# Permuting the closing factors inside SBUF, and two sums made by accumulating transfers, in a fused convolution and FFN kernel

## The chip, the cores and the metric

One Trainium2 chip, one of its cores. The metric is device time in microseconds: 2329.91 us is the median of three runs of the kernel before (2326.67 to 2331.57). The profiled execution, from which all rows below come, took 2344.11 us, of which 2342.3 us lie between its first and last instruction. About 0.2% is what a measurement of this kernel can tell from no change.

## The reference

Two stages run one after the other on 8 x 4096 = 32768 rows of 192 features.

```python
w = exp(weight_gen - max over K);  w = w / (sum over K + 1e-9)       # 8 heads, K = 7 taps
out[b, s, h, :] = sum over k of w[b, s, h, k] * x_pad[b, s + k, h, :] # 24 features a head, causal
h = out.reshape(32768, 192) @ w_in                                    # 192 -> 2048
g = max(h, 0) ** 2
y = g @ w_out                                                         # 2048 -> 192
```

## The kernel before, in words

The rows are cut into 64 chunks (`c`), each of 4 rows in each of 128 partitions. For a chunk the kernel makes the weighted sum over seven taps (the convolution), turns the result so that features lie in the partitions, splits it into a high and a low part, and runs the two matrix products with both parts, so that the result is close to float32.

**The convolution of a chunk** is VectorE work on tiles `pr` of 128x768: seven products (`mul`, L387) and six sums (`add`, L400). It is spread over the steps of the two chunks ahead of the one that uses it. `turn` (L488) transposes the sum in blocks of 32 into `xr`; four transfers on SyncE's queue write it to DRAM as `xd` (L494), two more read it back as `xT` in the layout wanted (L499). ScalarE then makes the high part `xh` (L428) and VectorE the low part `xl` (L431), three pieces each.

**A chunk's main loop** has eight steps `j`. In each step TensorE makes two blocks of the first product (`mm1`, L523) and two of the second (`mm2_scaled`, L604 to L614) for work that is two steps older. ScalarE does relu, square and the high part of the result, VectorE the low part (L560). At step 1 the second product of the chunk before ends. `sum_turned` then frees its four PSUM banks: ScalarE copies two of them, VectorE adds the other two (L651), part 0 first and part 1 later in the step. The second product of the next chunk cannot begin until these adds are done.

**Part 1** holds the last 64 features as two half sums, in partitions 0 to 63 and 64 to 127. L653 moves the upper half down by a transfer on SyncE's queue; at step 4 VectorE adds it (L667) and transposes the result (L668).

**The closing factor.** Chunks 6 to 62 are called scaled: their rows are scaled by powers of two, and at the end each output row is multiplied by a factor twice (`close_scaled`, L687). The factor is one number for each partition, made once for two chunks at step 2 of the even chunks (`factor`). As the output has its partitions permuted, so must the factor be: GpSimd's queue writes 128 numbers to a DRAM tile `fd` (L284), and when this has landed reads them back by four transfers in the other order (L288). The table `SCALED_SLOTS` says how many entries of the convolution's list each step takes, and `N_AHEAD` how many of them stand ahead of `sum_turned` at step 1.

**What sets the order.** Each engine and each queue runs its instructions in the order in which the program issues them. An instruction that waits holds all that is behind it on its engine or queue. Chunks 1 to 3 already let transfers accumulate (`moved`, L405).

Of the kernel before, what the change touches and what calls it, by code (L numbers as in the profile page):

```python
# [8 lines left out]
F32 = mybir.dt.float32  # L9
# [5 lines left out]
ALU = mybir.AluOpType  # L15
# [15 lines left out]
def kernel(  # L31
# [9 lines left out]
    nc = tc.nc  # L41
# [4 lines left out]
    P = 128  # L46
    Q = 32
# [8 lines left out]
    D1 = 64  # L56
# [6 lines left out]
    LAG = 2  # L63
    CONV_BEG = 1
    CONV_SLOTS = (2, 1, 4, 1, 3, 0, 3, 3, 0, 3)
    SCALED_SLOTS = (2, 1, 4, 1, 2, 1, 3, 2, 3, 1)
    OUT_STEP = 3
    LOAD_STEP = 5
    NBUF = NF // 2
    FIRST = 6  # L70
    GL_POOL = 5
    SCALE_STEP = NJ
    N_AHEAD = 3

    const = ctx.enter_context(tc.tile_pool(name="const", bufs=1))
    stage = ctx.enter_context(tc.tile_pool(name="stage", bufs=3))
# [4 lines left out]
    op = ctx.enter_context(tc.tile_pool(name="op", bufs=1))  # L81
    dram = ctx.enter_context(tc.tile_pool(name="dram", bufs=2, space=bass.MemoryType.DRAM))
# [6 lines left out]
    def put_out(c, t0, t1, o_sb, reads):  # L89
        rows = slice(rows_of(c) + t0, rows_of(c) + t1)  # L90
        if reads == 0:
            nc.sync.dma_start(out=out.rearrange("(p r) d -> p r d", r=R)[:, rows, :], in_=o_sb[:, t0:t1])
            return
        if reads == 3:
            v = out.rearrange("(q a b r) d -> b q a r d", q=P // Q, a=P // Q, r=R)
            n = v.shape[0] // 4
            for k in range(4):
                nc.sync.dma_start(out=v[k * n:(k + 1) * n, :, :, rows, :], in_=o_sb[k * Q:(k + 1) * Q, t0:t1])
            return
        v = out.rearrange("(q a b r) d -> q b a r d", q=P // Q, a=2 ** reads, r=R)  # L100
        for q in range(P // Q):
            nc.sync.dma_start(out=v[q, :, :, rows, :], in_=o_sb[q * Q:(q + 1) * Q, t0:t1])
# [7 lines left out]
    def is_scaled(c):  # L110
        return FIRST <= c < NCH - 1
# [167 lines left out]
    def factor(gi):  # L279
        f = att.tile([P, 1], F32, name="x_fac", bufs=2)  # L280
        x_out[gi] = fo = att.tile([P, 1], F32, name="x_out", bufs=3)
        nc.vector.tensor_tensor(out=f, in0=x_pow[gi], in1=v_unroot, op=ALU.mult)  # L282
        fd = dram.tile([P, 1], F32, name="fd")
        nc.gpsimd.dma_start(out=fd, in_=f)  # L284
        v = fd.rearrange("(q a b) e -> b q a e", q=P // Q, a=P // Q)
        n = v.shape[0] // 4
        for k in range(4):
            nc.gpsimd.dma_start(out=fo[k * Q:(k + 1) * Q], in_=v[k * n:(k + 1) * n])  # L288

    def peak_w(k):  # L290
        nc.vector.tensor_reduce(
# [37 lines left out]
    def conv_steps(c, on_pe, moving=False):  # L329
# [3 lines left out]
        n = TC * H  # L333
        wf = wt[:, lo:lo + TC].rearrange("p t h k -> p (t h) k")
        if c < N_PE:
            e = eps[c]
# [5 lines left out]
        parts = xts[c] = {}  # L342
# [28 lines left out]
        def product(k):  # L371
            if on_pe and k < 3:
                if "spare" not in parts:
                    parts["spare"] = att.tile([P, 2, TC, D], F32, name="spare", tag="xT")
                return att.tile([P, TC, D], F32, name="prx", tag="xr") if k == 2 else parts["spare"][:, k]
            if moving and k == 4:
                return att.tile([P, TC, D], F32, name="prw", tag="wide")
            return att.tile([P, TC, D], F32, name="pr", bufs=4)

        def mul(k, t0=0, t1=TC):  # L380
            def f():
                if k not in prs:
                    prs[k] = product(k)
                m = (t1 - t0) * H
                src = xt[:, lo + k + t0:lo + k + t1, :].rearrange("p t (h g) -> p (t h) g", h=H)
                dst = prs[k][:, t0:t1, :].rearrange("p t (h g) -> p (t h) g", h=H)
                tt(out=dst, in0=src, in1=wf[:, t0 * H:t1 * H, k:k + 1].broadcast_to([P, m, G]), op=ALU.mult)  # L387
            return f
# [9 lines left out]
        def add(k, k0=0):  # L398
            def f():
                tt(out=prs[k0], in0=prs[k0], in1=prs.pop(k), op=ALU.add)  # L400
            return f

        def moved(k, k0):
            def f():
                nc.gpsimd.dma_start(out=prs[k0], in_=prs.pop(k), accum_op=ALU.add)  # L405
            return f

        def both(*fs):
            return lambda: [f() for f in fs]

        def taps():
            if moving:
                return [mul(0), both(mul(1), moved(1, 0)), mul(2), both(mul(3), moved(3, 2)),
                        both(mul(4), moved(4, 0)), mul(5), mul(6), add(5, 6), add(2, 6), add(6)]
            fs = [mul(0), mul(1)]
            for k in range(1, K):
                if k + 1 < K:
                    fs.append(mul(k + 1))
                fs.append(add(k))
            return fs  # L420
# [60 lines left out]
        def turn():  # L481
# [16 lines left out]
            for h in range(2):  # L498
                nc.sync.dma_start(out=xT[h * D1:(h + 1) * D1], in_=xd.rearrange("(k p) n -> p k n", p=D1))  # L499

        return steps + taps() + [turn], splits


# [139 lines left out]
    def sum_turned(c, parts=(1, 0)):  # L643
        acc = accs[c]
        if c not in works:
            works[c] = stage.tile([P, 3, N], F32, name="raw")
        X = works[c]
        for k in parts:
            nc.scalar.copy(X[:, k], acc[2 * k])  # L649
        for k in parts:  # L650
            nc.vector.tensor_tensor(out=X[:, k], in0=acc[2 * k + 1], in1=X[:, k], op=ALU.add)  # L651
        if 1 in parts:
            nc.sync.dma_start(out=X[0:D1, 2], in_=X[D1:P, 1])  # L653

    def store_turned(c, part):
        X = works[c]

        def blocks(v):
            return v.rearrange("p (a t i) -> p t a i", a=P // Q, t=TC) if is_scaled(c) else v

        if part == 0:
            o_sb = op.tile([P, TC, D], F32, name="o_sb", bufs=2)
            Y = stage.tile([P, 2, N], F32, name="raw")
            outs[c] = o_sb, Y
            nc.vector.transpose(blocks(Y[:, 0]), X[:, 0])
        else:
            nc.vector.tensor_tensor(out=X[0:D1, 1], in0=X[0:D1, 1], in1=X[0:D1, 2], op=ALU.add)  # L667
            nc.vector.transpose(blocks(outs[c][1][0:D1, 1]), X[0:D1, 1])  # L668
        o_sb, Y = outs[c]
        y = Y[:, part].rearrange("p (t q i) -> p q t i" if c < N_PE or is_scaled(c) else "p (q t i) -> p q t i", t=TC, i=Q)  # L670
        for e in range(P // Q if part == 0 else D1 // Q):
            d0 = part * P + e * Q
            if is_scaled(c):
                nc.sync.dma_start(out=o_sb[:, :, d0:d0 + Q], in_=outs[c][1][e * Q:(e + 1) * Q, part])
                continue
            for q in range(P // Q):
                queue = nc.gpsimd if part and c == NCH - 2 else nc.sync
                queue.dma_start(
                    out=o_sb[q * Q:(q + 1) * Q, :, d0:d0 + Q],
                    in_=y[e * Q:(e + 1) * Q, q],  # L680
                )
        if part and not is_scaled(c):
            put_out(c, 0, TC, o_sb, 2)
# [150 lines left out]
    def plan_conv(m, a, b):  # L834
# [5 lines left out]
        elif m > 3:  # L840
            fs = iter(a)
            for j, n in enumerate(SCALED_SLOTS if is_scaled(m) else CONV_SLOTS):
                for _ in range(n):
# [20 lines left out]
    for gi in range(FIRST // CPG, NCH // CPG):  # L864
        at(CPG * gi - 2, 2, lambda gi=gi: measure(gi))
        at(CPG * gi - 2, 3, lambda gi=gi: power(gi))
        at(CPG * gi, 2, lambda gi=gi: factor(gi))
# [8 lines left out]
    for c in range(1, NCH):  # L876
        tail = c == NCH - 1
        for j in range(NJ):
# [28 lines left out]
            if split_sum:  # L907
                for f in fs[:N_AHEAD]:
                    f()
                del fs[:N_AHEAD]  # L910
                sum_turned(done, (0,))
            elif done is not None:
                sum_turned(done)
            for f in fs:
                f()
            if c > 1:
                for part in range(2):
                    if j == (LOAD_STEP if tail else 2 * part + 2 if is_scaled(c - 1) else OUT_STEP + part):
                        store_turned(c - 1, part)
# [4 lines left out]
            if split_sum:  # L924
                sum_turned(done, (1,))
# [5 lines left out]
    c = NCH - 1  # L931
# [56 lines left out]
```

## Time and profile before

| what | value |
|---|---|
| median of 3 runs | 2329.91 us |
| profiled execution | 2344.11 us |
| its span, first to last instruction | 2342.3 us |
| TensorE busy | 2151.8 us (92%) |
| VectorE busy | 1949.2 us (83%) |
| ScalarE busy | 1842.7 us (79%) |
| GpSimd busy | 95.6 us (4%) |
| mean granted TensorE clock | 0.973 |

A busy share is an average over stretches with different limits. A chunk's cycle is best cut at the start of its transpose `xr` (L488), which occurs once in each chunk. A row of a table of stretches has the stretch, its length, the busy time of each engine in it, the granted clock and the share of the DMA engines that was in use. SPq is SyncE's queue of transfers; a transfer's row has the time it was issued, not that it landed.

### The profile page before, as it was taken

To read this page: it belongs to the slowest core of one execution; us is meant where nothing else is said; L and a number is where in the kernel's file an instruction comes from. 1 tells how busy PE (TensorE), PEld (TensorE's weight loads), DVE (VectorE), ACT (ScalarE), POOL (GpSimd) and SP (SyncE) were. 2 spreads that over 40 slices of the span, in tenths; PEclk is the share of its full clock that TensorE was granted. 3 is DMA by queue.
4 is the path that set the end of the run, shared out by engine and by line. 5 is a ranking of instruction groups with operands and counts; after the bars stand their busy time and mean duration, and the time that the engine had idled before them with its cause. 6 is when DMAs were issued, how large, how long until landed. Compare 5 with 4: busy or idle time off the path is not lost.

```text
span 2342.3 us, 49184 instructions
## 1 busy us (share of the span) xinstructions
PE 2151.8 (92%) x19484; PEld 1735.2 (74%) x19484; DVE 1949.2 (83%) x3067; ACT 1842.7 (79%) x3551; POOL 95.6 (4%) x163
## 2 busy tenths in 40 slices
PE   9989899998999999998889988999898999989989
PEld 8878677777777777776767767677676777767778
DVE  9989887977879888788787887888878788888885
ACT  8878777877878777888777787787877878778786
POOL 1000000000000000000000000000000000000000
PEclk9999999999999999999999999999999999999999
DMA  8433334333243342433424334233342433423422
GB/s 214 93 84 65 91 71 97 80 86 72 70 95 80 87 91 56 88 86 89 92 53 85 87 87 92 53 84 89 84 92 53 85 91 85 89 60 78 95 52 57
DMA packets 311296, 195.47 MB, mean 83 GB/s; under 512 B 212000, under 2 KB 269472, under 8 KB 307224
## 3 DMA queue, kind: packets, MB, share of 16 engines
q1 hardware_dynamic: 305128, 188.64, 36.2%
q0 software_dynamic: 5936, 3.68, 1.1%
q8 instruction: 152, 2.49, 0.5%
q14 instruction: 80, 0.66, 0.1%
HBM read 106.54 MB, written 49.56 MB: 67 GB/s over the span
## 4 chain that ended last, share of the span: by engine, by line
DVE 43%; PE 26%; DMA 17%; ACT 5%; issue 5%; SPq 2%; DVEq 0%; another core or an unknown queue 0%; ACTq 0%
PE ph L523 14%; DVE pr L400 10%; DMA xT<-xd 9%; DVE pr L387 9%; DVE du L560 9%; DMA xd<-xr 7%; PE acc L604 6%; DVE xl L431 4%; DVE gl L560 4%; DVE raw L651 3%; PE acc L639 2%; ACT rg L540 2%; PE acc L608 1%; ACT xh L428 1%; ACT rg L547 1%
## 5 line engine op out<-in xcount | busy, mean ns | idle before, releaser
L523 PE MATMUL ph<-xh,W 64*128 64x512 f32 x6096 | 1066.0, 409 | 0.0
L604 PE MATMUL acc<-gh,V 64*128 64x512 f32 x5472 | 796.2, 393 | 160.2 <-DVE raw L651 83.2
L604 PEld LDWEIGHTS acc<-gh,V 64*128 64x128 f32 x5472 | 593.1, 191 | 276.6 <-DVE raw L651 120.6
L523 PEld LDWEIGHTS ph<-xh,W 64*128 64x128 f32 x6096 | 715.8, 190 | 100.2 <-ACT gh L551 13.2
L540 ACT ACTIVATE rg<-ph 128x512 f32<-128x512 f32 x992 | 538.6, 596 | 240.8 <-PE ph L523 234.2
L547 ACT ACTIVATE rg<-rg 128x512 f32<-128x512 f32 x1007 | 580.7, 634 | 0.2
L551 ACT CAST gh<-rg 128x512 fp32r<-128x512 f32 x1008 | 575.6, 625 | 3.0 <-PE acc L581 3.0
L523 PE MATMUL ph<-xl,W 64*128 64x512 f32 x3048 | 491.0, 380 | 0.1
L387 DVE TENSOR_TENSOR pr<-xt,wt 128x768 f32<-128x768 f32 x440 | 418.1, 952 | 2.3
L560 DVE TENSOR_TENSOR gl<-rg,gh 128x512 f16<-128x512 f32 x570 | 390.2, 741 | 25.9 <-ACT gh L551 24.4
L523 PEld LDWEIGHTS ph<-xl,W 64*128 64x128 f32 x3048 | 360.0, 189 | 40.9 <-ACT xl L442 0.5
L431 DVE TENSOR_TENSOR xl<-xT,xh 128x512 fp32r<-128x512 f32 x186 | 122.1, 686 | 305.6 <-ACT xh L428 300.9
L400 DVE TENSOR_TENSOR pr<-pr 128x768 f32<-128x768 f32 x366 | 348.9, 953 | 2.2
L428 ACT CAST xh<-xT 128x512 fp32r<-128x512 f32 x186 | 108.0, 618 | 195.1 <-DMA xT<-xd 195.1
L608 PE MATMUL acc<-gl,du 64*128 64x512 f16 x1140 | 237.3, 390 | 1.0 <-DVE gl L560 1.0
L560 DVE TENSOR_TENSOR du<-rg,gh 128x512 f16<-128x512 f32 x342 | 232.1, 733 | 2.4 <-ACT gh L551 2.4
L608 PEld LDWEIGHTS <-du 64*128 64x128 f16 x1824 | 100.1, 98 | 104.2 <-issue 57.7
L608 PE MATMUL acc<-du 64*128 64x512 f16 x684 | 132.9, 400 | 15.1 <-DVE du L560 14.4
L284 POOL DMA_DIRECT2D fd<-x_fac x29 | 17.1, 589 | 1874.9 <-DVE x_fac L282 1752.4
L614 PEld LDWEIGHTS <-du 64*64 64x64 f16 x1824 | 48.3, 106 | 57.8 <-issue 24.1
L651 DVE TENSOR_TENSOR raw<-acc,raw 128x512 f32<-128x512 f32 x124 | 84.4, 684 | 6.6 <-ACT raw L649 6.6
L649 ACT COPY raw<-acc 128x512 f32<-128x512 f32 x124 | 74.1, 601 | 14.0 <-PE acc L639 9.8
(127 smaller groups left out, 1230.1 us busy)
## 6 DMA issues: line engine op xcount, KB each, us to landing
xT<-xd SPq DMA_DIRECT2D x124, 384.0 KB
xt<-in_x_dram SPq DMA_DIRECT2D x30, 1344.0 KB
out_dram<-o_sb SPq DMA_DIRECT2D x254, 96.0 KB
xd<-xr SPq DMA_DIRECT2D x248, 96.0 KB
o_sb<-raw SPq DMA_DIRECT2D x342, 64.0 KB
raw<-raw SPq DMA_DIRECT2D x62, 128.0 KB
wt<-in_weight_gen_dram SPq DMA_DIRECT2D x31, 224.0 KB
raw<-in_moe_w_in_dram SPq DMA_DIRECT2D x16, 192.0 KB
```

The lines of the kernel that those rows point to most:

```text
L387: tt(out=dst, in0=src, in1=wf[:, t0 * H:t1 * H, k:k + 1].broadcast_to([P, m, G]), op=ALU.mult)
L400: tt(out=prs[k0], in0=prs[k0], in1=prs.pop(k), op=ALU.add)
L428: nc.scalar.copy(parts["h"][:, k, n], src[k][:, n])
L431: tt(out=parts["l"][:, k, n], in0=src[k][:, n], in1=parts["h"][:, k, n].bitcast(F32), op=ALU.subtract)
L523: nc.tensor.matmul(two[i], w, order(xx[rows, k]), start=(n == 0), stop=(n == last))
L540: nc.scalar.activation(r, ph, AF.Relu)
L547: nc.scalar.activation(r, r, AF.Square)
L551: nc.scalar.copy(gh, rgs[c, fb])
L560: nc.vector.tensor_tensor(out=gl, in0=g, in1=h, op=ALU.subtract)
L604: nc.tensor.matmul(acc[b + h], V[rows, fb, e:e + P], two_halves(g[rows]), start=fb == 0 and e < 2 * P, stop=False)
L608: nc.tensor.matmul(acc[h], V16[rows, 2 * j + i, 0:P], gls[c, j][rows, i], start=False, stop=last and i == 1)
L651: nc.vector.tensor_tensor(out=X[:, k], in0=acc[2 * k + 1], in1=X[:, k], op=ALU.add)
```

## The change

Three parts, all in the scaled chunks. The factor no longer goes through DRAM: eight transfers of 16 numbers each, on GpSimd's queue, read every eighth partition of `x_fac` and write 16 partitions of `x_out`. One of the six sums of the convolution (product 3 onto product 2) is made by an accumulating transfer on GpSimd's queue; the products 2 and 3 come first for that, and the list has 19 entries in place of 20. The upper half sum of part 1 is added to the lower by an accumulating transfer on GpSimd's queue; the transfer on SyncE's queue and VectorE's add go.

```diff
-    SCALED_SLOTS = (2, 1, 4, 1, 2, 1, 3, 2, 3, 1)
+    SCALED_SLOTS = (2, 1, 4, 1, 2, 1, 3, 2, 2, 1)
-    N_AHEAD = 3
+    N_AHEAD = 2
@@ factor
-        fd = dram.tile([P, 1], F32, name="fd")
-        nc.gpsimd.dma_start(out=fd, in_=f)
-        v = fd.rearrange("(q a b) e -> b q a e", q=P // Q, a=P // Q)
-        n = v.shape[0] // 4
-        for k in range(4):
-            nc.gpsimd.dma_start(out=fo[k * Q:(k + 1) * Q], in_=v[k * n:(k + 1) * n])
+        n = P // (P // Q) ** 2
+        for b in range(n):
+            nc.gpsimd.dma_start(out=fo[b * P // n:(b + 1) * P // n], in_=f[b::n])
@@ taps
+            if is_scaled(c):
+                return [mul(2), both(mul(3), moved(3, 2)), mul(0), mul(1), add(1), mul(4), add(4), mul(5), add(5), add(2), mul(6), add(6)]
@@ sum_turned
-        if 1 in parts:
+        if 1 in parts and is_scaled(c):
+            nc.gpsimd.dma_start(out=X[0:D1, 1], in_=X[D1:P, 1], accum_op=ALU.add)
+        elif 1 in parts:
             nc.sync.dma_start(out=X[0:D1, 2], in_=X[D1:P, 1])
@@ store_turned
-            nc.vector.tensor_tensor(out=X[0:D1, 1], in0=X[0:D1, 1], in1=X[0:D1, 2], op=ALU.add)
+            if not is_scaled(c):
+                nc.vector.tensor_tensor(out=X[0:D1, 1], in0=X[0:D1, 1], in1=X[0:D1, 2], op=ALU.add)
```

The line numbers in the changed kernel differ by a few: L387 is now L384, L400 is L397, L405 is L402, L431 is L430, L488 is L487, L494 is L493, L499 is L498, L560 is L559, L651 is L650, L653 is L652 (on GpSimd's queue in the scaled chunks), L668 is L670, L674 is L676, L687 is L689, L288 is L285.

VectorE between a transpose `xr` and the first low part `xl`, from the first product of the next convolution on (`gl` is the low part of the result, `raw` holds the output sums). Before:

```order
L387 TENSOR_TENSOR pr<-xt,wt 128x768
L560 TENSOR_TENSOR gl<-rg,gh 128x2x256 x2
L387 TENSOR_TENSOR pr<-xt,wt 128x768
L667 TENSOR_TENSOR raw<-raw 64x512
L668 STREAM_TRANSPOSE raw<-raw 64x4x4x32
L560 TENSOR_TENSOR gl<-rg,gh 128x2x256 x2
L431 TENSOR_TENSOR xl<-xT,xh 128x512
```

After:

```order
L384 TENSOR_TENSOR pr<-xt,wt 128x768
L559 TENSOR_TENSOR gl<-rg,gh 128x2x256 x2
L384 TENSOR_TENSOR pr<-xt,wt 128x768
L670 STREAM_TRANSPOSE raw<-raw 64x4x4x32
L559 TENSOR_TENSOR gl<-rg,gh 128x2x256 x2
L430 TENSOR_TENSOR xl<-xT,xh 128x512
```

The add of the half sums is gone; the two products are now 2 and 3 in place of 0 and 1, and the second is followed by the accumulating transfer on GpSimd's queue.

VectorE from the closing multiplication at step 0 to the two adds that free the PSUM banks. Before:

```order
L687 TENSOR_SCALAR o_sb<-o_sb,x_out 128x768
L387 TENSOR_TENSOR pr<-xt,wt 128x768
L400 TENSOR_TENSOR pr<-pr 128x768
L560 TENSOR_TENSOR gl<-rg,gh 128x2x256 x2
L387 TENSOR_TENSOR pr<-xt,wt 128x768
L400 TENSOR_TENSOR pr<-pr 128x768 x2
L651 TENSOR_TENSOR raw<-acc_16560,raw 128x512
L356 TENSOR_REDUCE mx<-wt 128x32
L357 TENSOR_TENSOR wt<-wt,mx 128x224
L651 TENSOR_TENSOR raw<-acc_16562,raw 128x512
```

After:

```order
L689 TENSOR_SCALAR o_sb<-o_sb,x_out 128x768
L397 TENSOR_TENSOR pr<-pr 128x768 x2
L559 TENSOR_TENSOR gl<-rg,gh 128x2x256 x2
L384 TENSOR_TENSOR pr<-xt,wt 128x768
L397 TENSOR_TENSOR pr<-pr 128x768
L650 TENSOR_TENSOR raw<-acc_16561,raw 128x512
L353 TENSOR_REDUCE mx<-wt 128x32
L354 TENSOR_TENSOR wt<-wt,mx 128x224
L650 TENSOR_TENSOR raw<-acc_16563,raw 128x512
```

One sum less stands ahead of the adds that free the banks; in step 0 a product and a sum have become two sums.

GpSimd's queue where the first scaled chunks begin (the rows on `pr`, `prw` are those of chunks 1 to 3). Before:

```order
L405 DMA pr<-prw 128x768
L405 DMA pr<-pr 128x768 x2
L405 DMA pr<-prw 128x768
L284 DMA fd<-x_fac 128x1
L288 DMA x_out<-fd 32x1x1 x4
```

After:

```order
L402 DMA pr<-prw 128x768
L402 DMA pr<-pr 128x768 x2
L285 DMA x_out<-x_fac 16x1 x8
L402 DMA pr<-pr 128x768
L652 DMA raw<-raw 64x512
L402 DMA pr<-pr 128x768
```

The queue that held five small transfers for two chunks now holds eight small ones, and an accumulating transfer of 128x768 and one of 64x512 for each chunk. From SyncE's queue only L653 is gone, in each scaled chunk; what follows it there, `xd` and `xT`, is in the same order.

## Rows read from the trace of the kernel before

**Rows 1.** The page: the chain that ended last, share of the span.
```profile
DVE 43%; PE 26%; DMA 17%; ACT 5%; issue 5%; SPq 2%; DVEq 0%; another core or an unknown queue 0%; ACTq 0%
```
**Rows 2.** Busy time by stretch: length, engines, granted clock, DMA share, GB/s.
```profile
1006.45:1039.65 33.20, 32.33 (x309) 26.07 (x305) 30.02 (x47) 27.38 (x52) 0.00 (x0) 1.00 0.46 113
1039.65:1078.71 39.06, 32.81 (x307) 25.85 (x305) 30.35 (x50) 29.79 (x59) 2.95 (x5) 1.00 0.29 55
1078.71:1111.38 32.67, 32.07 (x309) 26.11 (x305) 30.14 (x47) 26.94 (x52) 0.00 (x0) 1.00 0.47 115
243.00:2247.11 2004.11, 1829.68 (x16683) 1452.97 (x16680) 1666.78 (x2588) 1574.02 (x3031) 82.76 (x140) 0.97 0.37 81
```
**Rows 3.** SyncE's queue in order of time: start, time to issue, transfer.
```profile
131.94 1.79 SPq L494 DMA_DIRECT2D xd<-xr  x4
136.74 1.33 SPq L499 DMA_DIRECT2D xT<-xd  x2
...
244.06 2.42 SPq L494 DMA_DIRECT2D xd<-xr  x4
254.63 1.31 SPq L499 DMA_DIRECT2D xT<-xd  x2
...
1040.67 2.69 SPq L494 DMA_DIRECT2D xd<-xr  x4
1051.32 1.28 SPq L499 DMA_DIRECT2D xT<-xd  x2
...
1079.71 1.80 SPq L494 DMA_DIRECT2D xd<-xr  x4
1083.25 1.29 SPq L499 DMA_DIRECT2D xT<-xd  x2
...
2208.97 2.11 SPq L494 DMA_DIRECT2D xd<-xr  x4
2219.92 1.28 SPq L499 DMA_DIRECT2D xT<-xd  x2
```
**Rows 4.** GpSimd in order of time, the even chunk's stretch; in brackets the wait before.
```profile
1040.05 0.59 POOL L284 DMA_DIRECT2D fd<-x_fac  x1 [61.25 <-DVE x_fac L282]
1049.40 2.36 POOL L288 DMA_DIRECT2D x_out<-fd  x4 [8.76 <-issue]
```
**Rows 5.** Busy time by stretch, inside the even chunk's stretch.
```profile
1045.00:1050.50 5.50, 5.50 (x54) 4.67 (x51) 5.07 (x8) 4.45 (x9) 1.10 (x2) 1.00 0.00 0
```
**Rows 6.** VectorE in order of time; in brackets the wait before an instruction.
```profile
1058.50 0.69 DVE L431 TENSOR_TENSOR xl<-xT,xh 128x512 fp32r<-128x512 f32 x1 [8.40 <-ACT xh L428]
...
1085.05 0.97 DVE L387 TENSOR_TENSOR pr<-xt,wt 128x768 f32<-128x768 f32 x1
...
1090.98 0.69 DVE L431 TENSOR_TENSOR xl<-xT,xh 128x512 fp32r<-128x512 f32 x1 [2.29 <-ACT xh L428]
...
1092.46 0.95 DVE L400 TENSOR_TENSOR pr<-pr 128x768 f32<-128x768 f32 x1
1093.33 1.35 DVE L560 TENSOR_TENSOR du<-rg,gh 128x512 f16<-128x512 f32 x2
```
**Rows 7.** The chain that ended last, in order of time: start, length, what.
```profile
1011.65 6.98 DMA xT<-xd
...
1051.99 5.78 DMA xT<-xd
```
**Rows 8.** Groups by line: count, busy us, mean ns, idle before.
```profile
L667 DVE TENSOR_TENSOR raw<-raw 64x512 f32<-64x512 f32 x62 | 42.2, 681 | 5.0 <-DMA raw<-raw 5.0
```
**Rows 9.** GpSimd in order of time: the last accumulating transfer of the early chunks.
```profile
84.85 0.86 POOL L405 DMA_DIRECT2D pr<-prw  x1 [3.95 <-DVE prw L387]
```
**Rows 10.** Busy time by stretch, around that transfer.
```profile
86.00:88.50 2.50, 2.50 (x28) 2.19 (x26) 2.47 (x5) 1.97 (x5) 0.00 (x0) 1.00 0.87 157
88.50:89.00 0.50, 0.50 (x8) 0.45 (x6) 0.50 (x1) 0.50 (x2) 0.00 (x0) 1.00 0.00 0
```
**Rows 11.** Who waited for whom, stretch 1078.7 to 1111.4.
```profile
PE acc L604 <- DVE raw L651: 0.6, 1, 0.6
```

## The prediction

> **What bounds the kernel now.** The page's chain comes first: it changes between VectorE (43%), TensorE (26%) and transfers (17%), so no engine bounds alone [rows 1]. I therefore cut the span into the stretches between two transposes `xr`, and the table of stretches shows two kinds in turn. The one that starts in an even chunk takes 39.06 us, its neighbours 33.20 and 32.67 us, though the engines do nearly the same work in each: TensorE 32.81, 32.33 and 32.07 us, VectorE 30.35, 30.02 and 30.14 us [rows 2]. In the short kind TensorE stands still for 32.67 - 32.07 = 0.6 us, and that is its wait for the adds that free the PSUM banks [rows 2, 11]. The short stretch is bound by TensorE; the long one has some 6 us in which nobody is the bound.
>
> Where these 6 us go is read in the queues. In the short stretch the reading of `xT` is issued 3.54 us after the first writing of `xd` (1079.71 to 1083.25), in the long one 10.65 us after it (1040.67 to 1051.32). The first and the last of the 28 long stretches have 10.57 and 10.95 us [rows 3]. SyncE waits there for `xd` to be reported as landed. But the DMA engines move nothing from 1045.0 to 1050.5 [rows 5]: the bytes are through, the report is late. What lies beside it in the even chunks alone is the factor's way through DRAM: `fd` is issued at 1040.05, just ahead of `xd`, and GpSimd sees it landed only at 1049.40, 9.35 us later, for 512 bytes [rows 4]. Chunk 4 is even and has no factor yet: 4.80 us from `xd` to `xT` (131.94 to 136.74) [rows 3]. So I take the write of 128 numbers of 4 bytes to DRAM to be what holds back the reports of `xd`. VectorE pays: it waits 8.40 us for `xl` in the long stretch and 2.29 us in the short one [rows 6].
>
> **The change part by part.**
>
> *Factor.* `fd` goes, in 29 chunks (6, 8, ... 62). If it is the cause, all 28 long stretches become like the short ones. In its place stand eight issues. Four of the old ones took 2.36 us [rows 4], so eight take some 4.7 us of an engine that is 4% busy, from about 1040 to 1045; the next work on that queue is the accumulating transfer after the second product, some 7 us after the transpose. The factor is used first a chunk later. Cost on the path: nothing, if these transfers don't hold up `xd` as `fd` does. They write 4 bytes at a time too, but to SBUF. The nearest row is the four `x_out` transfers, which also write 4 bytes to SBUF: they were issued from 1049.40 to 1051.76, `xT` at 1051.32, and `xT` then took 5.78 us in the chain against 6.98 us where no such transfer was near [rows 3, 4, 7]. So between 0 (by this) and 7 us a long stretch (as `fd`); I take 0.
>
> The Trainium skill, DMA: Bandwidth & Descriptors, section Specifications, gives 512 bytes as the least transfer for full rate and says that anything smaller is done by read-modify-write. By that rule the eight new transfers would be in the same class as `fd`; the two `xT` times above speak against it for SBUF, and the first rival below has its result.
>
> *The convolution's sum.* One add less for VectorE, 0.87 us from start to start in a row of such instructions (1092.46 to 1093.33) [rows 6], and it is one of those between `xl` and the adds that free the banks, so it is on the path from `xl` to the next transpose. Added is a transfer of 384 KB that reads, adds and writes. Its own cost is seen in an early chunk: issued at 84.85, it moved from about 86.0 to before 88.5 [rows 9, 10], so some 3.7 us with 2.2 us of all DMA engines at the 0.87 share. Issued at 1086.02, where the second product ends [rows 6], it is done by about 1090. Its sum is needed only at step 0 of the next chunk, and the tile that it reads is written again by a product of step 7, which comes after the rows shown to 1093.33 + 1.35 = 1094.68 [rows 6]. That cover is over 4 us; without it VectorE would wait for what is over. What it can hit is `xT`: issued at 1083.25, landing some 7 us later [rows 3, 7], so its last 3 us lie beside the accumulation's 2.2 us from about 1087.2. Bounds: 0 and 2.2 us later for `xT`. The bytes of `xT` are the earlier of the two, so I take 0.7 us, of which VectorE's and TensorE's slack (below) leaves little.
>
> *The half sum.* L667 goes, 0.68 us for each chunk [rows 8], but it stands before the wait for `xl` [rows 6]: it turns into waiting, gain 0. The transfer changes to GpSimd's queue and accumulates 128 KB, a third of the one above. It is issued right after the second add that frees the banks, two instructions ahead of the transpose, and the transpose of part 1 that waits for it comes after the product that ends at 1086.02, over 7 us after `xr`. At 3.7 us it is hidden twice over. If it came later than that, VectorE's idle 2.29 us would take the first of it. On SyncE's queue one wait goes ahead of `xd`; `xd` waits for a later VectorE instruction, so nothing is gained.
>
> *The sum.* From the first `xr` in chunk 6 (243.0) to that in chunk 61 (2247.1) lie 55 stretches in 2004.1 us, 36.4 us each, 28 long and 27 short [rows 2]. The new stretch P has two floors. TensorE: 32.07 us. VectorE and the transfers: 12.27 us from `xr` to `xl` (1078.71 to 1090.98) and 20.40 from there to the next `xr` (1111.38) [rows 2, 6], less 0.87: 31.8 us, or 32.5 with the 0.7 us. The wait for the banks, 0.6 us, shrinks with the add that stood ahead of it. I take P = 32.5 us. 55 x 32.5 = 1787.5, which is 216.6 us less. The profiled execution would be 2344.1 - 216.6 = 2127.5 us; it stands 0.6% above the median of the runs (2329.9 / 2344.1 = 0.9939), so the forecast is 2115 us. In the 55 stretches the mean granted clock is 0.97, in the short ones shown 1.00, which is 2.4 GHz throughout [rows 2]; that part of the gain is in P already.
>
> The likeliest case alone: P from 32.07 (TensorE without any wait: 1763.9, so 2103.9, at the median 2091 us) to 33.4 us (1837, so 2177, at the median 2164 us), the short stretch of today with some collision and no gain by the add.
>
> **The rivals.**
>
> *The eight small transfers hold `xd` as `fd` did.* For it: 4 bytes each, the same queue, issued at the same moment as `xd`. Against it: `xT` beside `x_out`, and the target is not DRAM. Then only the add is gained: 0.87 us in 28 long stretches and some 0.5 us in 27 short ones, 38 us: 2306, at the median 2292 us.
>
> *The accumulation takes its full 2.2 us from `xT`.* For it: both run over the same DMA engines and the times touch. Against it: most of `xT` is through by then. P = 31.8 + 2.2 = 34.0 us, 55 x 34.0 = 1870, 134 us less: 2210, at the median 2197 us.
>
> *Slower: the accumulation of the half sum, in flight just ahead of `xd` in every chunk, holds back its report.* Price: the 7.1 us of the long stretch, now in all 55. P = 31.8 + 7.1 = 38.9 us, 2140 us, 135 us more: 2480, at the median 2465 us. It is slower than before from P = 36.4 us on, a delay of 4.6 us a chunk. Against it: in the early chunk the DMA engines are idle 3.7 us after the issue [rows 9, 10], and it writes to SBUF in pieces of 2 KB. The Trainium skill, same page, section Queues, rings and completion order, says that a report is a write that lands only after every earlier write of that DMA engine, across its queues. By that rule the report of `xd` waits for whatever GpSimd's queue has in flight: it is what `fd` shows, and the way by which this rival would come.
>
> **How the numbers follow.** Forecast 0.77, the full collision 0.11, the small transfers 0.07, slower 0.04, and 0.01 that all cancels. The forecast's own range is 2091 to 2164 us. With the collision (2197) it holds 88%, of which some part lies outside: 2085 to 2197 us as the range. Faster by over 0.2%, which is about what a measurement of this kernel can tell from no change: 0.95 (the first three cases); within 0.2%: 0.01; slower: 0.04.
>
> **What would show it.** Right: no more alternation, all stretches near 32.5 us, `xT` issued 3.5 to 5 us after `xd` in even chunks too, no 8 us wait of VectorE for `xl`, TensorE busy about 98% in the stretches. VectorE's adds (now L397) 57 fewer. The step on the factor is wrong if even chunks keep 10 us between `xd` and `xT`; the step on the accumulation is wrong if VectorE's wait for `xl` is above 4 us in all chunks; the step on the half sum is wrong if VectorE waits ahead of the transpose L670. The forecast fails if TensorE, without its long pause, is not fed at the rate of the short stretches.

## The result, and the profile after

The changed kernel takes 2101.8 us (median of four runs, 2101.0 to 2104.7), the kernel before 2328.3 us (median of four): a ratio of the means of 0.9035, with a 95% interval of 0.9007 to 0.9063. The forecast was 2115 us, with 2091 to 2164 us for the likeliest case. The profiled execution has a span of 2100.0 us, 242.3 us less than before.

The page of the changed kernel, its busy times and its chain that ended last:

```profile
PE 2074.4 (99%) x19484; PEld 1707.0 (81%) x19484; DVE 1870.8 (89%) x2953; ACT 1845.2 (88%) x3551; POOL 221.2 (11%) x364
...
PE 71%; DVE 15%; DMA 6%; ACT 4%; issue 2%; SPq 1%; DVEq 0%; ACTq 0%
```

The chain that alternated between VectorE, TensorE and transfers [rows 1] is now for 71% TensorE's own work. The table of stretches of the changed kernel, from one `xr` to the next (L487), has first all 55, then an even chunk, an odd one and an even one; the columns are those of [rows 2], the busy times in the order TensorE, its weight loads, VectorE, ScalarE, GpSimd:

```profile
239.90:2007.30 1767.40, 1757.42 (x16693) 1429.36 (x16692) 1591.98 (x2479) 1574.68 (x3028) 204.04 (x334) 1.00 0.48 103
1075.01:1106.93 31.92, 31.92 (x307) 25.98 (x304) 29.17 (x49) 29.23 (x57) 5.64 (x10) 1.00 0.41 79
1106.93:1139.48 32.55, 32.09 (x310) 26.16 (x306) 28.73 (x45) 28.47 (x56) 1.72 (x2) 1.00 0.53 128
1139.48:1171.43 31.95, 31.92 (x307) 25.99 (x304) 29.06 (x48) 28.87 (x56) 5.63 (x10) 1.00 0.43 80
```

The 39 us of the even chunk are gone: it is now even a little shorter than its neighbour. The 55 stretches take 1767.4 us in place of 2004.1 [rows 2], 32.13 us each; these 236.7 us are nearly all of the 242.3. In them TensorE is busy for 1757.4 us, 99.4%, at a granted clock of 1.00 (2.4 GHz), where the mean was 0.97 before.

SyncE's queue in the changed kernel, an even chunk and an odd one:

```profile
1076.00 1.81 SPq L493 DMA_DIRECT2D xd<-xr  x4
1080.09 1.29 SPq L498 DMA_DIRECT2D xT<-xd  x2
...
1107.92 1.81 SPq L493 DMA_DIRECT2D xd<-xr  x4
1112.89 1.28 SPq L498 DMA_DIRECT2D xT<-xd  x2
```

and GpSimd's, in the same stretches:

```profile
1075.38 3.88 POOL L285 DMA_DIRECT2D x_out<-x_fac  x8 [0.49 <-DVE x_fac L282]
1084.35 0.92 POOL L402 DMA_DIRECT2D pr<-pr  x1 [5.09 <-DVE pr L384]
1106.07 0.84 POOL L652 DMA_DIRECT2D raw<-raw  x1 [20.80 <-DVE raw L650]
1114.51 0.90 POOL L402 DMA_DIRECT2D pr<-pr  x1 [7.60 <-DVE pr L384]
```

In the even chunk eight small transfers go out beside `xd`, and `xT` follows 4.09 us after it, where it was 10.65 [rows 3]. Over the even chunks of the trace the median is 3.92 us (10.93 before), over the odd ones 3.66; the 4.97 us of the odd chunk shown are the longest of these. What waits is seen in three rows of the list of waits over the whole span: who, for whom, in all, times, the longest:

```profile
DVE xl L430 <- ACT xh L427: 121.8, 59, 3.3
...
ACT xh L427 <- DMA xT<-xd: 8.6, 22, 0.9
...
PE acc L603 <- DVE raw L650: 8.4, 22, 0.6
```

No wait for `xl` is longer than 3.3 us any more (one of 8.40 stands in [rows 6]), `xT` is hardly ever what ScalarE waits for, and TensorE stands 8.4 us in all for the adds that free the banks. The last two of these rows were, before:

```profile
ACT xh L428 <- DMA xT<-xd: 195.1, 40, 7.6
PE acc L604 <- DVE raw L651: 83.2, 83, 2.1
```

### The profile page after: what moved, and what is told of

Read it like the earlier page. It is cut to its first block, busy times and chain, and to the rows that moved or that the text cites. A ratio compares the mean times of both kernels' runs of the same rounds, so it can differ in the third digit from the quotient of the medians.

```text
span 2100.0 us, 49532 instructions
## 1 busy us (share of the span) xinstructions
PE 2074.4 (99%) x19484; PEld 1707.0 (81%) x19484; DVE 1870.8 (89%) x2953; ACT 1845.2 (88%) x3551; POOL 221.2 (11%) x364
## 4 chain that ended last, share of the span: by engine, by line
PE 71%; DVE 15%; DMA 6%; ACT 4%; issue 2%; SPq 1%; DVEq 0%; ACTq 0%
PE ph L522 38%; PE acc L603 21%; DMA xT<-xd 4%; PE acc L607 4%; PE acc L613 4%; DVE pr L384 4%; DVE du L559 3%; DVE pr L397 3%; PE acc L638 3%; DVE xl L430 2%; DVE raw L650 1%; DVE gl L559 1%; ACT rg L539 1%; PE acc L570 1%; ACT rg L546 1%
## 5 line engine op out<-in xcount | busy, mean ns | idle before, releaser
L603 PE MATMUL acc<-gh,V 64*128 64x512 f32 x5472 | 772.9, 378 | 10.1 <-DVE raw L650 8.4
L559 DVE TENSOR_TENSOR gl<-rg,gh 128x512 f16<-128x512 f32 x570 | 389.6, 740 | 47.4 <-ACT gh L550 47.4
L384 DVE TENSOR_TENSOR pr<-xt,wt 128x768 f32<-128x768 f32 x440 | 412.3, 949 | 2.3
L397 DVE TENSOR_TENSOR pr<-pr 128x768 f32<-128x768 f32 x309 | 295.2, 955 | 6.1
L559 DVE TENSOR_TENSOR du<-rg,gh 128x512 f16<-128x512 f32 x342 | 232.0, 732 | 3.7 <-ACT gh L550 3.7
L607 PE MATMUL acc<-gl,du 64*128 64x512 f16 x1140 | 230.8, 381 | 1.0 <-DVE gl L559 1.0
L430 DVE TENSOR_TENSOR xl<-xT,xh 128x512 fp32r<-128x512 f32 x186 | 122.2, 687 | 122.0 <-ACT xh L427 121.8
L652 POOL DMA_DIRECT2D raw<-raw x57 | 47.3, 830 | 1261.3 <-DVE raw L650 1170.6
L607 PE MATMUL acc<-du 64*128 64x512 f16 x684 | 138.2, 382 | 0.0
L285 POOL DMA_DIRECT2D x_out<-x_fac x232 | 112.3, 493 | 42.5 <-DVE x_fac L282 41.4
L402 POOL DMA_DIRECT2D pr<-pr x63 | 57.0, 905 | 531.3 <-DVE pr L384 484.8
```

What stands on the lines that cost most here:

```text
L285: nc.gpsimd.dma_start(out=fo[b * P // n:(b + 1) * P // n], in_=f[b::n])
L430: tt(out=parts["l"][:, k, n], in0=src[k][:, n], in1=parts["h"][:, k, n].bitcast(F32), op=ALU.subtract)
L559: nc.vector.tensor_tensor(out=gl, in0=g, in1=h, op=ALU.subtract)
L603: nc.tensor.matmul(acc[b + h], V[rows, fb, e:e + P], two_halves(g[rows]), start=fb == 0 and e < 2 * P, stop=False)
L607: nc.tensor.matmul(acc[h], V16[rows, 2 * j + i, 0:P], gls[c, j][rows, i], start=False, stop=last and i == 1)
```

## The experiments

All times are medians; each ratio is of the means, to runs of the kernel before on the same chip. These differ by chip: 2324 us for e1 to e4, 2348 us for e5 to e8, 2343 us for e9 to e12. The stretches are those of the profiled execution of each kernel.

| kernel | us | ratio, 95% interval | 55 stretches, us | each |
|---|---|---|---|---|
| e1 factor alone | 2139.4 | 0.9210 (0.9193 to 0.9226) | 1800.3 | 32.73 |
| e2 convolution's sum alone | 2292.8 | 0.9870 (0.9841 to 0.9898) | 1960.4 | 35.64 |
| e3 half sum alone | 2320.8 | 0.9989 (0.9976 to 1.0002) | | |
| e4 both sums, factor by DRAM | 2285.8 | 0.9831 (0.9813 to 0.9849) | 1950.0 | 35.45 |
| e5 factor by DRAM, later | 2142.0 | 0.9117 (0.9101 to 0.9132) | 1804.5 | 32.81 |
| e6 written once only | 2147.9 | 0.9145 (0.9127 to 0.9162) | | |
| e7 written 512 bytes apart | 2142.7 | 0.9124 (0.9106 to 0.9142) | 1806.9 | 32.85 |
| e8 written from SyncE's queue | 2328.8 | 0.9908 (0.9876 to 0.9940) | 1980.1 | 36.00 |
| e9 factor and convolution's sum | 2103.3 | 0.8974 (0.8958 to 0.8990) | 1766.0 | 32.11 |
| e10 factor and half sum | 2141.1 | 0.9136 (0.9120 to 0.9152) | 1803.4 | 32.79 |
| e11 written 64 bytes apart | 2141.9 | 0.9139 (0.9123 to 0.9155) | 1803.2 | 32.79 |
| e12 the changed kernel again | 2106.5 | 0.8990 (0.8973 to 0.9007) | | |

**Which part makes the gain (e1 to e4).** Theory 1: the write of `fd` held back the report on `xd`. Rival 2: the relief of VectorE made the gain. Rival 3: either part alone makes about half of it.

e1 is the kernel before with this and nothing else:

```diff
-        fd = dram.tile([P, 1], F32, name="fd")
-        nc.gpsimd.dma_start(out=fd, in_=f)
...
+        n = P // (P // Q) ** 2
+        for b in range(n):
+            nc.gpsimd.dma_start(out=fo[b * P // n:(b + 1) * P // n], in_=f[b::n])
```

> The kernel before with the factor's part alone: eight transfers inside SBUF, no write to DRAM; both sums stay on VectorE. Theory 1 (the write of 128 numbers to DRAM held back the report that xd had landed): xT is issued some 3.6 us after xd in all chunks, all stretches between two transposes take 32.5 to 33.0 us, so about 2115 to 2145 us. Rival 2 (VectorE's relief by 0.87 + 0.68 us a chunk made the gain; the pause in even chunks would have gone with it): alternation stays at about 39 and 33 us, 2300 to 2330 us. Rival 3 (either part alone gives about half): about 2215 us.

e2 takes the new order of taps and the accumulating transfer:

```diff
-    SCALED_SLOTS = (2, 1, 4, 1, 2, 1, 3, 2, 3, 1)
+    SCALED_SLOTS = (2, 1, 4, 1, 2, 1, 3, 2, 2, 1)
...
-    N_AHEAD = 3
+    N_AHEAD = 2
...
+            if is_scaled(c):
+                return [mul(2), both(mul(3), moved(3, 2)), mul(0), mul(1), add(1), mul(4), add(4), mul(5), add(5), add(2), mul(6), add(6)]
```

> The kernel before with one convolution sum made by an accumulating transfer and nothing else; the factor still goes through DRAM. Theory 1: even chunks keep 10 to 12 us from xd to xT; the add is gained where VectorE is on the path, 0.5 to 0.9 us in each of 55 stretches, 28 to 48 us, so 2280 to 2300 us. Rival 2: most of the 226 us, below 2200 us.

e3 takes the half sum:

```diff
-        if 1 in parts:
+        if 1 in parts and is_scaled(c):
+            nc.gpsimd.dma_start(out=X[0:D1, 1], in_=X[D1:P, 1], accum_op=ALU.add)
+        elif 1 in parts:
...
-            nc.vector.tensor_tensor(out=X[0:D1, 1], in0=X[0:D1, 1], in1=X[0:D1, 2], op=ALU.add)
+            if not is_scaled(c):
+                nc.vector.tensor_tensor(out=X[0:D1, 1], in0=X[0:D1, 1], in1=X[0:D1, 2], op=ALU.add)
```

> The kernel before with the half sum of the last features made by an accumulating transfer and nothing else. Theory 1, by the step that L667 stands ahead of a wait for xl: 0 us gained, 2320 to 2332 us; VectorE waits 0.7 us longer for xl in each chunk. If the accumulation held back xd's report it would be slower by up to 135 us. Rival 2: faster by 20 us or more.

e4 is e2 and e3 together, that is, the changed kernel with `fd` back in DRAM.

> The changed kernel with the factor put back through DRAM: both sums by transfers, fd still written. Theory 1: the pause is back, even stretches about 38.5 us, odd ones about 32.5 us, about 2280 to 2300 us. Rival 2: close to the changed kernel, 2100 to 2150 us. Rival 3: about 2215 us.

Measured: e1 alone has 7.9 of the 9.65%, within what theory 1 gave. e4 has 1.7%. e2 gives 1.3% and e3 nothing that can be told from zero. Rivals 2 and 3 are out. The trace of e4, SyncE's queue, an even chunk and an odd one, shows the pause unchanged while both sums are by transfers:

```profile
1022.75 2.24 SPq L496 DMA_DIRECT2D xd<-xr  x4
1031.90 1.29 SPq L501 DMA_DIRECT2D xT<-xd  x2
...
1059.74 1.78 SPq L496 DMA_DIRECT2D xd<-xr  x4
1063.32 1.29 SPq L501 DMA_DIRECT2D xT<-xd  x2
```

9.15 us against 3.58; the medians of the trace are 9.71 and 3.64. In e1 TensorE is left with a wait for the adds that free the banks; the row of the list of waits, and the line of all 55 stretches:

```profile
PE acc L601 <- DVE raw L648: 36.8, 61, 1.1
```
```profile
243.66:2043.98 1800.32, 1761.52 (x16687) 1424.48 (x16684) 1666.64 (x2589) 1578.01 (x3030) 107.30 (x224) 1.00 0.40 90
```

**What it is in `fd` (e5 to e8, e11).** In e5 the factor is made four steps later, with all of its transfers as before:

```diff
-        at(CPG * gi, 2, lambda gi=gi: factor(gi))
+        at(CPG * gi, 6, lambda gi=gi: factor(gi))
```

> The kernel before, with the factor made at step 6 of the even chunk in place of step 2: the write to DRAM and the four reads are as they were, only no longer in flight together with xd. If it is the neighbourhood of fd and xd that costs: the pause goes, xT 3.6 us after xd in all chunks, 2130 to 2160 us, as with the factor's part alone. If something else about even chunks (the squares on ScalarE, the loads) made the pause: 2310 to 2330 us. If the late report hits whatever transfer is near, for example the stores and loads of steps 5 to 8: between, 2160 to 2300 us.

It takes as long as the factor alone inside SBUF does (32.81 us a stretch against 32.73). GpSimd's rows of e5 show that `fd` is nearly as slow as ever, 8.44 us from 1047.51 to 1055.95, though no `xd` is beside it:

```profile
1047.51 0.59 POOL L284 DMA_DIRECT2D fd<-x_fac  x1 [53.34 <-DVE x_fac L282]
1055.95 2.38 POOL L288 DMA_DIRECT2D x_out<-fd  x4 [7.84 <-issue]
```

So neither the other work of even chunks nor the way through DRAM as such makes the pause: it is that `fd` was in flight together with `xd`.

In e6 `fd` is written in chunk 6 only; 28 writes are left out, so the later chunks use the first factor:

```diff
-        fd = dram.tile([P, 1], F32, name="fd")
-        nc.gpsimd.dma_start(out=fd, in_=f)
+        if not fds:
+            fds.append(dram.tile([P, 1], F32, name="fd", bufs=1))
+            nc.gpsimd.dma_start(out=fds[0], in_=f)
+        fd = fds[0]
```

> The kernel before, with fd written once, for chunk 6, and only read afterwards: 28 writes are left out, so the later chunks use the first factor. The reads of 4 bytes from DRAM to SBUF stay and now start at once, beside xd. If the write holds xd's report: 2130 to 2160 us. If reads of 4 bytes, or any small transfer from GpSimd's queue, do it as well: 2300 us or more.

The pause is gone but in chunk 6, where `fd` is still written: there `xT` follows `xd` after 10.12 us and the stretch takes 38.70 us, the only one above 33.6 us in the trace.

```profile
243.03 2.86 SPq L497 DMA_DIRECT2D xd<-xr  x4
253.15 1.31 SPq L502 DMA_DIRECT2D xT<-xd  x2
```

The reads did not start beside `xd`, as was expected: with no write ahead of them they waited for their buffer, until the closing multiplication (`o_sb`), as GpSimd's row shows:

```profile
1059.11 2.35 POOL L291 DMA_DIRECT2D x_out<-fd  x4 [62.25 <-DVE o_sb L690]
```

So e6 says that without the write there is no pause, and nothing on the reads.

In e7 the numbers lie 512 bytes apart, in e11 64 bytes (a row of 16 in place of 128):

```diff
-        fd = dram.tile([P, 1], F32, name="fd")
-        nc.gpsimd.dma_start(out=fd, in_=f)
+        fd = dram.tile([P, 128], F32, name="fd")
+        nc.gpsimd.dma_start(out=fd[:, 0:1], in_=f)
...
+        v = fd.rearrange("(q a b) e -> b q a e", q=P // Q, a=P // Q)[:, :, :, 0:1]
```

> The kernel before, with the 128 numbers of fd written 512 bytes apart in DRAM in place of side by side. If it is the many small writes into the same few bytes that queue for each other: fd lands in about 2 us, the pause goes, 2130 to 2160 us. If each write of 4 bytes to DRAM is slow by itself: as before, 2310 to 2330 us.

> The kernel before, with the 128 numbers of fd written 64 bytes apart in DRAM, 8 KB in all. If the writes queue for each other only within some 64 bytes or less: as with 512 bytes apart, no pause, 2130 to 2160 us. If it takes 512 bytes or a page of DRAM: a pause of 2 to 7 us in even chunks, 2180 to 2330 us.

Both are free of the pause. GpSimd's and SyncE's rows, in e7 and then in e11:

```profile
1034.40 0.59 POOL L284 DMA_DIRECT2D fd<-x_fac  x1 [60.20 <-DVE x_fac L282]
1037.34 2.38 POOL L288 DMA_DIRECT2D x_out<-fd  x4 [2.35 <-issue]
...
1035.02 1.81 SPq L494 DMA_DIRECT2D xd<-xr  x4
1038.46 1.38 SPq L499 DMA_DIRECT2D xT<-xd  x2
```
```profile
1030.47 0.59 POOL L284 DMA_DIRECT2D fd<-x_fac  x1 [59.37 <-DVE x_fac L282]
1033.45 2.38 POOL L288 DMA_DIRECT2D x_out<-fd  x4 [2.38 <-issue]
...
1031.09 1.81 SPq L494 DMA_DIRECT2D xd<-xr  x4
1034.56 1.45 SPq L499 DMA_DIRECT2D xT<-xd  x2
```

The same 128 numbers, written by the same queue at the same moment beside `xd`, are seen landed 2.94 and 2.98 us after their issue, against 9.35 side by side [rows 4], and `xT` follows `xd` after 3.44 and 3.47 us. And here the four transfers that read 4 bytes at a time do run beside `xT`, at no cost that the stretches show (32.85 and 32.79 us, against 32.73 in e1). One thing changes with the distance: the tile in DRAM grows from 512 bytes to 64 and 8 KB, and may lie elsewhere. No run has a tile of that size with the numbers side by side.

e8 writes `fd`, side by side, from SyncE's queue:

```diff
-        nc.gpsimd.dma_start(out=fd, in_=f)
+        nc.sync.dma_start(out=fd, in_=f)
```

> The kernel before, with fd written from SyncE's queue in place of GpSimd's, still 128 numbers side by side, just ahead of xd. If the kind of write counts and not the queue: the pause stays, 10 to 12 us from xd to xT in even chunks, 2310 to 2340 us. If GpSimd's queue is the cause: 2130 to 2160 us.

The pause stays. SyncE's rows of e8:

```profile
1031.74 0.34 SPq L284 DMA_DIRECT2D fd<-x_fac  x1
1032.63 2.58 SPq L494 DMA_DIRECT2D xd<-xr  x4
1043.29 1.28 SPq L499 DMA_DIRECT2D xT<-xd  x2
```

10.66 us from `xd` to `xT` (9.72 in the median of the even chunks), and 36.00 us a stretch. So it is the kind of write, not the queue that issues it. It is 0.9% faster than before; the reason is not known.

**What the sums are worth once the pause is gone (e9, e10, e12).** e9 is e1 with the convolution's sum of e2, e10 is e1 with the half sum of e3; e12 is the changed kernel, on the same chip. (The difference that the expectation of e9 starts from is that of the spans of e1 and the changed kernel, 2137.5 - 2100.0 = 37.5 us; the 139 us in it are no measured number.)

> The changed kernel with the half sum back on VectorE and SyncE's queue. The factor alone left TensorE waiting 36.8 us for the adds that free the banks, of 139 us that the factor alone did not gain or lose against the changed kernel's 2100 us span only some 37 us remain. If the convolution's sum alone is what brings them: within 3 us of the changed kernel. If the half sum has a part: 5 to 20 us slower than it.

> The changed kernel with the convolution's sum back on VectorE. If the half sum is worth nothing, as the prediction had it, within 3 us of the factor alone, that is some 37 us slower than the changed kernel; if the half sum has a part, less.

> The changed kernel once more, on the same chip as the other three, so that differences of less than one per cent can be read: 0.90 of the kernel before.

e9 is 3.2 us faster than the changed kernel, e10 34.7 us slower. The convolution's sum has the whole of the rest; the half sum gains nothing and may cost some 0.1%, which these runs don't settle (the intervals of e9 and e12 overlap). e9 has one accumulating transfer a chunk less than the changed kernel; its row for TensorE's wait:

```profile
PE acc L603 <- DVE raw L650: 7.6, 21, 0.6
```

against 36.8 us in e1 and 8.4 us in the changed kernel. These 28 to 29 us are most of the 34 us by which the stretches of e9 and e1 differ.

## Why the prediction was right

**The pause and its cause.** Right, and by the step given: the alternation is gone, and e1, e4, e5, e7 and e8 show that `fd` beside `xd` made it. One of its readings is wrong. It took the `xd` at 131.94 for that of chunk 4; that stretch is chunk 3's, an odd one, and chunk 4's is

```profile
172.69 1.80 SPq L494 DMA_DIRECT2D xd<-xr  x4
176.22 1.32 SPq L499 DMA_DIRECT2D xT<-xd  x2
```

With 3.53 us in place of 4.80 it says the same, and more clearly: an even chunk without a factor has no pause. What the prediction had not seen is why the write was slow. It named 4 bytes at a time; e11 shows that 4 bytes at a time, 64 bytes apart, are landed in 3 us. It is the 128 writes side by side in 512 bytes. The prediction's reason for trusting the eight new transfers, that `x_out` beside `xT` cost nothing, held for the time: in e1 `xT` follows `xd` after 3.94 us in the median of the even chunks and 3.56 in the odd ones, and the even stretches are no longer for these 0.4 us (medians 32.58, and 32.61 in e5). The rule of the Trainium skill (DMA: Bandwidth & Descriptors, section Specifications) that anything under 512 bytes is done by read-modify-write does not by itself bring the pause: e7 and e11 are under it too.

**What is still open in it.** How `fd` delays `xd` is not settled. The Trainium skill, same page, section Queues, rings and completion order, has a report land only after every earlier write of its DMA engine, across the queues; that agrees with e8 and with the order of the events (`fd` landed at 1049.40, `xT` issued at 1051.32 [rows 3, 4]). But both `fd` and `xd` go to DRAM, and the bytes of `xd` could have been waiting there as well. That cannot be all, for in e4 a transfer inside SBUF is held too: the half sum `raw`, issued on GpSimd's queue 1.33 us ahead of `fd`. GpSimd's rows of e4, then VectorE's transpose that needs `raw`, then the table of a stretch just ahead of it:

```profile
1020.80 0.81 POOL L655 DMA_DIRECT2D raw<-raw  x1 [23.30 <-DVE raw L653]
1022.13 0.61 POOL L284 DMA_DIRECT2D fd<-x_fac  x1 [0.52 <-DVE x_fac L282]
1030.84 2.42 POOL L288 DMA_DIRECT2D x_out<-fd  x4 [8.09 <-DMA fd<-x_fac]
...
1030.39 0.70 DVE L673 STREAM_TRANSPOSE raw<-raw 64x512 f32<-64x512 f32 x1 [0.33 <-DMA raw<-raw]
...
1026.50:1030.30 3.80, 3.80 (x38) 3.25 (x36) 3.49 (x6) 3.44 (x8) 0.00 (x0) 1.00 0.00 1
```

VectorE has `raw` 9.6 us after its issue, 0.45 us before the reads that wait for `fd` start, and from 1026.50 to 1030.30 the DMA engines' share is 0.00, so its bytes were through. In the changed kernel, which has the same transfer and no `fd`, it is landed after 3.4 to 5.0 us in every chunk. In e4 it is late in most even chunks but not in all: of the ten whose landing the trace gives, seven took 7.6 to 10.3 us and three 3.8 to 5.4; in e3, where it is mostly landed after 3.1 us, two of eighteen took 9.2 and 10.1. As `raw` was issued ahead of `fd`, a rule on earlier writes does not by itself explain that; what holds the reports stays open.

**The floor.** Right in kind: TensorE. The stretch is 32.13 us, close to the prediction's floor of TensorE, 32.07. The 32.5 us that it took were the other of its two floors, that of VectorE and the transfers, with 0.7 us in it that did not come (below). The difference of 0.37 us in each of 55 stretches is 20 us, and the head and the tail, counted at nothing, gave 5.6 us more: the span was forecast 25.7 us too long (2342.3 - 216.6 = 2125.7 against 2100.0). Half of that was cancelled by luck: by the proportion of the kernel before the median was taken to lie 10.7 us below the span, and it lies 1.8 us above it. So the 13 us between forecast and result hide an error of twice their size.

**The mis-sized term** is the 0.7 us by which the accumulation was to delay `xT`. It did not come. In the chain of the changed kernel a transfer `xT` stands with 5.45 us, and before there were 5.78 and 6.98 [rows 7]:

```profile
1113.57 5.45 DMA xT<-xd
```

ScalarE waits 8.6 us in all for `xT`. The accumulation itself was slower than the early chunk had shown; the page's list of transfers (count, size, median us from issue to landing) has

```profile
pr<-pr POOLq DMA_DIRECT2D x63, 384.0 KB, 5.8
...
raw<-raw POOLq DMA_DIRECT2D x57, 128.0 KB, 3.9
```

5.8 us for the one that was put at 3.7 (six of the 63 are of the early chunks). So of the two it is the accumulation that is longer beside the other, not `xT`; that `xT` is what makes it longer is not shown, for the transfers to `o_sb` run beside it too. Its cover, put at over 4 us, was enough with what lies beyond the rows shown: VectorE's only wait for such a transfer is one of 0.6 us at 48.28, before the scaled chunks.

**The convolution's sum.** Right. VectorE has 57 adds fewer: its row now has 309, where the page of before, the second line here, counts 366.

```profile
L397 DVE TENSOR_TENSOR pr<-pr 128x768 f32<-128x768 f32 x309 | 295.2, 955 | 6.1
...
L400 DVE TENSOR_TENSOR pr<-pr 128x768 f32<-128x768 f32 x366 | 348.9, 953 | 2.2
```

Their worth is 31.5 us with the pause (e2 against the kernel before, 2324.3 - 2292.8) and 37.8 us without it (e10 against e9, 2141.1 - 2103.3). The prediction's first rival had 38 us for it with the pause, and its forecast 0.87 us of VectorE's floor in each stretch. What it relieves without the pause is TensorE's wait for the adds that free the banks (e1 against e9), which the prediction had shrinking from 0.6 us.

**The half sum.** Right: nothing (e3, and e9 against e12). The row of the transpose that now waits for the transfer in place of the add has hardly any idle time before it, where L667 had 5.0 us [rows 8]:

```profile
L670 DVE STREAM_TRANSPOSE raw<-raw 64x512 f32<-64x512 f32 x62 | 43.3, 698 | 0.2
```

**The rivals.** The small transfers did not hold `xd` as `fd` did (e1, 0.4 us). The collision did not come. The slower case, the half sum's accumulation just ahead of `xd`, did not come: e3 has it with nothing else changed and is not slower. The clock came back to 1.00 with the pauses gone, as taken.

## What to carry to other kernels

When busy shares alternate from stretch to stretch with the same work in each, look for the time in which no engine is the bound, and in it for the transfer whose report is late though the DMA engines stand still; then ask what else was in flight, however small. Here 512 bytes written as single numbers side by side in DRAM took 9.35 us to be seen landed, and cost some 6 us in every second chunk; moving them inside SBUF, spreading them or issuing them at another time each took that away (e1, e11, e5). And a relief of an engine is worth what stands between it and the next wait of the bound: the one add ahead of the freeing of the banks had 38 us, the other, ahead of a wait for a transfer, none.

## What was not expected of the hardware

128 writes of 4 bytes from SBUF to DRAM, side by side in 512 bytes, took 9.35 us from issue until GpSimd saw them landed [rows 4]; 64 or 512 bytes apart, 2.98 and 2.94 us. While they were in flight, the report on another queue's 384 KB to DRAM came some 7 us late, with the DMA engines at a share of 0.00 from 1045.0 to 1050.5 [rows 5]. Issued from SyncE's queue they had the same effect: 10.66 us from `xd` to `xT`. A transfer inside SBUF that was issued 1.33 us ahead of them came late too, 9.6 us after its issue in place of about 4 (e4).
